# Threshold attention and a SoLU feed-forward on one core: three transfers for the weights' blocks, k and v loaded into all 128 rows

## The chip, the core and the metric

The kernel runs on one core of a Trainium2 chip. The metric is the device time of one execution in microseconds (us). Three executions of the kernel before gave 881.29, 881.4 and 883.73 us; the median, 881.4 us, is what the changed kernel is compared with.

The engines have short names here, as in the profile: PE is TensorE's matmul, PEld its load of the stationary operand, DVE is VectorE, ACT is ScalarE, POOL is GpSimd, SP is SyncE, which issues nearly all DMAs. A queue's name ends in q (SPq).

## The reference, cut to what matters

```python
# q, k, v: (8, 8, 576, 64) float32; tau = 0.02
scores = 0.125 * np.matmul(q, k.transpose(0, 1, 3, 2))
thresh = np.max(scores, axis=-1, keepdims=True) - tau
scores = np.where(scores >= thresh, scores, -1e9)
attn = np.exp(scores - np.max(scores, axis=-1, keepdims=True))
attn = attn / (np.sum(attn, axis=-1, keepdims=True) + 1e-09)
attn_out = np.matmul(attn, v)
x = attn_out.transpose(0, 2, 1, 3).reshape(4608, 512)
h = x @ w_in                         # (4608, 1024)
e = np.exp(h - np.max(h, axis=-1, keepdims=True))
solu = h * (e / (np.sum(e, axis=-1, keepdims=True) + 1e-9))
mu = np.mean(solu, axis=-1, keepdims=True)
var = np.mean((solu - mu) ** 2, axis=-1, keepdims=True)
out = (((solu - mu) / np.sqrt(var + 1e-6)) * g_ln) @ w_out   # (4608, 512)
```

## The kernel before

**Slots and rounds.** There are 8 batches (`b`) of 8 heads. Two heads make a pair; `NP` = 4 pairs per batch, numbered `hp`, and pair `i` is `b * NP + hp`. The 576 queries of a head are cut into two kinds of 256 (`kind` 0 and 1) and a rest of 64 (`kind` 2). A slot is one 128-row block of scores for both heads of a pair, and a batch has `PER` = 18 of them: 8 of kind 0, 8 of kind 1 and 2 of kind 2. One loop runs over rounds; a round issues, for all engines, the scores of one slot and whatever else is due. The order on each engine is the order in which this loop writes the instructions (the manual schedule), and each engine runs its queue strictly in order. Dates are in rounds: "round `PER * b - 9`" is nine rounds before the first slot of batch b.

**Attention of a slot.** PE makes the scores in PSUM (L451, tiles `s_ps`, one buffer for each head). DVE finds the row limit (L473), ACT makes the threshold ramp and the exponential (L488, L497), POOL normalises the rows (L504 to L507), and DVE transposes 32x32 blocks of the weights into `T` (L519). When both slots of a unit are in `T`, four DMAs on SP move the blocks from `T` to `wT` (L527 to L530), each from 32 partitions to 64 rows. Three rounds after the unit's second slot PE multiplies `wT` with `v` (L555, "pv"), and ACT copies the result into the tokens `xh`.

**Feed-forward.** A tile of 128 tokens takes `ff_h` (L611) and `ff_o` (L715) on PE, and between them DVE, ACT and POOL work and four DMAs on SP from `u` to `V` (`ff_swap`, L693), after which DVE makes `uT` (L703). A tile is begun about every fourth round.

**Inputs.** `q` is loaded for four heads at a time (L130) and turned by PE: `turn` (L312) multiplies with the identity matrix `ident`; `q_item` (L340) asks for it. For batches 0 and 1, `k` is turned the same way. From batch 2 on `load_natural` (L179) brings the `k` of one pair by four DMAs of 32 rows each (L186), `turn_natural` (L188) has DVE transpose it into `flip` (L191), and two DMAs put it into `kT` (L194). `v` of batches from 2 on is loaded by four DMAs for each half of a batch (L158), each two heads into 64 rows; rows 0 to 63 and 64 to 127 of `v` hold the same data, because PE uses both halves (`ROWS`). The rounds of these loads are worked out in L791 to L807. In batch 0 the sixteen pieces of `w_in` and `w_out` are also loaded as 64-bit numbers (L248) and turned into float32 by DVE, ACT and POOL (L259 to L298).

**Queues.** SP issues a round's DMAs in this order: `ff_swap` of the round, `wT` blocks of the slot before, output stores, `kT` halves, weight pieces, then `k`, `q` and `v` loads. A DMA whose input isn't ready holds back all behind it on SP. PE's order in a round is: the turns that ride on this slot, the scores, a quarter of the feed-forward, then pv.

## Time and profile before

| | |
|---|---|
| median of three runs | 881.4 us |
| the profiled execution's own time | 883.54 us |
| its span, first to last instruction | 881.8 us |
| mean granted TensorE clock | 0.980 |
| DMAs that SP issues: `wT`, `V`, `k`, `kT`, `v` | 288, 144, 96, 48, 48 (and 12 older `v` loads) |

The page's own head gives for each engine the time in which it was busy, and then the span in 40 equal slices of 22 us, one digit (tenths) a slice. The groups of instructions say how often a form ran, its mean time, and what ended the idle time just before it. Three of the groups around the change:

```profile
L519 DVE STREAM_TRANSPOSE T<-w 128x576 f32<-128x576 f32 x288 | 206.3, 752 | 7.4 <-POOL w L507 6.0
L703 DVE STREAM_TRANSPOSE uT<-V 128x1024 f32<-128x1024 f32 x36 | 44.5, 1236 | 23.7 <-DMA V<-u 23.5
L488 ACT ACTIVATE w<-s_ps,nth 128x576 f32<-128x576 f32 x280 | 199.8, 743 | 97.0 <-DVE nth L473 93.1
```

The first row reads: 288 transposes of 0.752 us took 206.3 us of DVE's span, and DVE stood idle for 7.4 us just before them, most of it until POOL had written the weights.

DVE's transpose of `k` (L191) takes 0.732 us. On SP, issuing took a median of 0.62 us for one `wT` DMA (mean 0.91), 0.45 (0.73) for one of `k`, 0.64 (0.94) for one of `v`, 0.58 (0.63) for one of `kT`. [...]

### The profile page before, as it was taken

How to read it: one execution, taken by the hardware profiler on the slowest of the kernel's cores; microseconds unless marked ns; L12 is line 12 of the kernel's file. 1: busy time of each engine (PE TensorE's matmuls, PEld its weight loads, DVE VectorE, ACT ScalarE, POOL GpSimd, SP SyncE). 2: the span in 40 equal slices, each digit the busy share in tenths (PEclk: the TensorE clock that was granted, in tenths of full speed). 3: DMA queues.
4: the chain of work that ended last, by engine and by line, in shares of the span. 5: the costliest groups of instructions: out<-in, count | busy, mean ns of one | idle time of the engine just before them, and what ended most of it. 6: DMA issues, size and time to landing. Idle time of an engine off the chain costs nothing. (4 is left out here: it accounts for less than half of the span.)

```text
span 881.8 us, 38016 instructions
## 1 busy us (share of the span) xinstructions
PE 835.4 (95%) x16225; PEld 592.1 (67%) x16225; DVE 682.0 (77%) x1248; ACT 586.3 (66%) x1201; POOL 471.0 (53%) x888
## 2 busy tenths in 40 slices
PE   5667999989999999999999999999999999999997
PEld 3445666665676877677777777777677677777655
DVE  5989788878787888888778887888687888777451
ACT  5977777767666766767677677777676777775121
POOL 2878655545555555555554655555555555555120
PEclk9878899999999999999999999999999999999999
DMA  7999978887878796988789787888779777866222
GB/s 230 254 260 256 218 186 196 217 191 175 201 170 212 178 208 157 206 207 189 158 194 214 184 204 166 208 213 185 165 173 219 182 174 155 186 133 143 65 49 49
DMA packets 85033, 161.60 MB, mean 183 GB/s; under 512 B 19832, under 2 KB 49536, under 8 KB 84864
## 3 DMA queue, kind: packets, MB, share of 16 engines
q1 hardware_dynamic: 83728, 157.18, 76.6%
q8 instruction: 127, 2.08, 1.1%
q10 hardware_dynamic: 1136, 2.00, 0.7%
q14 instruction: 42, 0.34, 0.1%
HBM read 46.14 MB, written 9.44 MB: 63 GB/s over the span
## 5 line engine op out<-in xcount | busy, mean ns | idle before, releaser
L473 DVE CUSTOM_DVE_ANT_0 w<-s_ps,tau_t 128x576 f32<-128x576 f32 x280 | 200.7, 754 | 108.0 <-PE s_ps L451 90.7
L715 PE MATMUL o_ps<-w,uT 64*64 64x256 f32 x4608 | 265.2, 376 | 1.1 <-DVE uT L703 1.1
L488 ACT ACTIVATE w<-s_ps,nth 128x576 f32<-128x576 f32 x280 | 199.8, 743 | 97.0 <-DVE nth L473 93.1
L715 PEld LDWEIGHTS o_ps<-w,uT 64*64 64x64 f32 x4608 | 218.9, 133 | 58.3 <-issue 13.8
L507 POOL TENSOR_SCALAR w<-w,sm 128x576 f32<-128x576 f32 x288 | 218.8, 772 | 14.3
L497 ACT ACTIVATE w<-w,ntau 128x576 f32<-128x576 f32 x288 | 220.3, 772 | 0.0
L611 PE MATMUL h_ps<-w,xh 64*64 64x512 f32 x1856 | 220.0, 596 | 0.0
L519 DVE STREAM_TRANSPOSE T<-w 128x576 f32<-128x576 f32 x288 | 206.3, 752 | 7.4 <-POOL w L507 6.0
L555 PEld LDWEIGHTS pv<-wT,v 64*64 64x64 f32 x5760 | 166.5, 136 | 51.1 <-issue 36.3
L451 PE MATMUL s_ps<-kT,qT 64*64 64x64 f32 (+1 forms) x2048 | 168.1, 422 | 16.4 <-ACT w L488 12.5
L555 PE MATMUL pv<-wT,v 64*64 64x128 f32 (+1 forms) x5760 | 170.9, 263 | 7.9 <-DMA wT<-T 3.7
L611 PEld LDWEIGHTS h_ps<-w,xh 64*64 64x64 f32 x1856 | 98.3, 135 | 96.6 <-issue 88.6
L504 POOL TENSOR_SCALAR sm<-sm 128x2 f32<-128x2 f32 x144 | 36.0, 250 | 229.5 <-ACT w L497 226.4
L505 POOL TENSOR_TENSOR sm<-sm,mone 128x2 f32<-128x2 f32 x144 | 104.6, 726 | 12.0
L677 ACT ACTIVATE V<-u,nb,rs 128x1024 f32<-128x1024 f32 x36 | 44.7, 1241 | 52.2 <-POOL nb L667 52.2
L451 PEld LDWEIGHTS s_ps<-kT,qT 64*64 64x64 f32 x2048 | 61.8, 139 | 25.1 <-ACT w L488 17.7
L578 ACT COPY xh<-pv 128x256 f32<-128x256 f32 x64 | 23.7, 370 | 67.3 <-PE pv L555 67.3
L703 DVE STREAM_TRANSPOSE uT<-V 128x1024 f32<-128x1024 f32 x36 | 44.5, 1236 | 23.7 <-DMA V<-u 23.5
L497 ACT ACTIVATION_READ_ACCUMULATOR w<-w,ntau 128x1 f32 x288 | 56.9, 198 | 0.0
L635 ACT ACTIVATE u<-h_ps,hm 128x1024 f32<-128x1024 f32 x36 | 40.2, 1118 | 21.2 <-DVE hm L626 15.3
L626 DVE TENSOR_REDUCE hm<-h_ps 128x1 f32<-128x1024 f32 x36 | 43.1, 1197 | 12.2 <-PE h_ps L611 6.2
L682 DVE TENSOR_SCALAR u<-u,rs,nb 128x1024 f32<-128x1024 f32 x36 | 42.4, 1178 | 12.7 <-ACT V L677 12.4
(82 smaller groups left out, 590.4 us busy)
## 6 DMA issues: line engine op xcount, KB each, us to landing
wT<-T SPq DMA_DIRECT2D x288, 288.0 KB, 5.9
v<-in_v_dram SPq DMA_DIRECT2D x48, 288.0 KB, 4.8
V<-u SPq DMA_DIRECT2D x144, 64.0 KB, 4.1
out_dram<-ob SPq DMA_DIRECT2D x71, 128.0 KB, 3.1
q<-in_q_dram SPq DMA_DIRECT2D x15, 512.0 KB, 5.9
k<-in_k_dram SPq DMA_DIRECT2D x96, 72.0 KB, 4.6
kT<-flip SPq DMA_DIRECT2D x48, 144.0 KB, 2.7
raw<-in_moe_w_out_dram SPq DMA_DIRECT2D x8, 512.0 KB, 8.2
```

Of the source, the lines that this page charges most:

```text
L451: nc.tensor.matmul(out=ps[h][ROWS[y], ks], lhsT=lhsT, rhs=d["kT"][ROWS[h], ks], start=True, stop=True,)
L473: nc.vector.tensor_tensor_reduce(out=w, in0=ps[:, 0:S], in1=(zero if loose else tau_t).to_broadcast([P, S]), scale=1.0, scalar=BIG, op0=AL ...
L488: nc.scalar.activation(out=d["w"][x], in_=d["w"][x] if d["loose"] else d["ps"][x][:, 0:S], func=AF.Prelu, bias=d["nth"][x], scale=-1.0, al ...
L497: nc.scalar.activation(out=w, in_=w, func=AF.Exp, bias=ntau, scale=1.0, accum_out=sm[:, x : x + 1])
L505: nc.gpsimd.tensor_tensor(out=sm, in0=sm, in1=mone, op=ALU.pow)
L507: nc.gpsimd.tensor_scalar(out=w, in0=w, scalar1=sm[:, x : x + 1], scalar2=1.0, op0=ALU.mult, op1=ALU.mult)
L519: nc.vector.transpose(out=T[:, :, r, h, :], in_=w)
L555: nc.tensor.matmul(out=to, lhsT=d["v"][ROWS[u], h0 + h, m ^ 4 * u if m < 8 and b < 2 else m], rhs=rhs, start=m == 0, stop=m == NK - 1,)
L611: mm = nc.tensor.matmul(out=h[ROWS[y], f], lhsT=x[ROWS[r], c, ROWS[y]], rhs=w1_parts[ROWS[r], c, part ^ r], start=part == 0 and c == 0, st ...
L677: nc.scalar.activation(out=V, in_=u, func=AF.Identity, bias=nb, scale=rs)
L703: nc.vector.transpose(out=uT, in_=d["V"].rearrange("p y (m x) -> p m y x", x=32))
L715: nc.tensor.matmul(out=d["o"][ROWS[z], 512 * r : 512 * r + 256], lhsT=d["uT"][ROWS[r], m].rearrange("p y x -> p (y x)"), rhs=w2[ROWS[r], m ...
```

## The change

Three things are changed.

1. **Blocks of weights.** For kinds 0 and 1 the four DMAs from `T` to `wT` become three: one takes partitions 32 to 95 and fills all 128 rows of `wT[:, 1]`, and two of 32 partitions fill the halves of `wT[:, 0]`. For this the 32-column halves of the queries of the second row half are exchanged: `turn` multiplies them with a new matrix `swapped` (two copies of `ident`'s blocks by POOL at the start) in place of `ident`. Kind 2 keeps its four DMAs.
2. **k from batch 2 on.** One DMA loads half the tokens (`a`) of two pairs into all 128 rows, 24 DMAs in place of 96. DVE's transposes stay 24, and the DMAs into `kT` 48; each transpose now serves half of two pairs. The rounds become `PER * b` - 9, - 7 (first two pairs) and - 1, + 1 (last two), with the loads three rounds before. Before they were - 13, - 9, - 5, - 1 for even batches from 4 on, - 11, - 7, - 3, + 1 for odd ones, and rounds 24, 30, 34, 39 for batch 2.
3. **v from batch 2 on.** Still four DMAs for a half batch, but of 576, 288, 144 and 144 KB in place of four of 288 KB: the first fills all rows for heads 0 and 2 (rows 64 to 127 get heads 1 and 3), the second one head slot with heads 1 and 2, the last two the rest. The matmul pv picks the head slot `(h0 + h - u) % 4`. The rounds are as before, but for one of the second half that moves from +6 to +5.

```diff
+    swapped = const.tile([P, 64], F32, name="swapped")
...
         if b > 1:
             if 0 in parts:
                 d["v"] = loads.tile([P, 4, NK, D], F32, tag="v", bufs=3, name="v")
+            to = d["v"].rearrange("p h m d -> p h (m d)")
+            rows = v_rows[64 * (H * b + 4 * hf) :][0:256]
             for part in parts:
-                two, u = divmod(part, 2)
-                nc.sync.dma_start(
-                    out=d["v"][ROWS[u], 2 * two : 2 * two + 2].rearrange("p h m d -> p h (m d)"),
-                    in_=v[b, hs][2 * two : 2 * two + 2].rearrange("h (p m) d -> p h (m d)", m=NK),
-                )
+                nc.sync.dma_start(**(
+                    dict(
+                        out=to.rearrange("p (e o) n -> p o e n", o=2)[:, 0],
+                        in_=rows.rearrange("(e r) n -> r e n", e=2),
+                    ),
+                    dict(out=to[:, 1], in_=rows[64:192]),
+                    dict(out=to[ROWS[1], 3], in_=rows[0:64]),
+                    dict(out=to[ROWS[0], 3], in_=rows[192:256]),
+                )[part])
             return
...
-    def load_natural(i):
-        b, hp = divmod(i, NP)
-        src = k[b, 2 * hp : 2 * hp + 2].rearrange("h (i a t) d -> a h i (t d)", a=2, t=NK)
+    k_rows = k.rearrange("b h (i a t) d -> a (b h i) (t d)", a=2, t=NK)
+    v_rows = v.rearrange("b h (p m) d -> (b h p) (m d)", m=NK)
+
+    def load_natural(i, a):
         raw = loads.tile([P, 4, 4, D], F32, tag="k", name="k")
-        natural[i] = raw = raw.rearrange("p h t d -> p (h t d)")[:, 0 : NK * D]
-        for g in range(4):
-            a, h = divmod(g, 2)
-            nc.sync.dma_start(out=raw[32 * g : 32 * g + 32], in_=src[a, h])
-
-    def turn_natural(i):
-        raw = natural.pop(i)
+        natural[i, a] = raw = raw.rearrange("p h t d -> p (h t d)")[:, 0 : NK * D]
+        nc.sync.dma_start(out=raw, in_=k_rows[a, 64 * i : 64 * i + P])
+
+    def turn_natural(i, a):
+        raw = natural.pop((i, a))
...
-        for a in range(2):
+        for j in range(2):
             nc.sync.dma_start(
-                out=to[:, 32 * NK * a : 32 * NK * (a + 1)],
-                in_=flip[ROWS[a]].rearrange("p g t x -> p g (t x)"),
+                out=pair(i + j)["kT"][:, 32 * NK * a : 32 * NK * (a + 1)],
+                in_=flip[ROWS[j]].rearrange("p g t x -> p g (t x)"),
             )
...
         make_identity(nc, ident)
+        for g in range(2):
+            of = 64 + 32 * (1 - g)
+            nc.gpsimd.tensor_copy(
+                out=swapped[ROWS[1], 32 * g : 32 * g + 32], in_=ident[ROWS[1], of : of + 32]
+            )
...
-                    out=spare[r][ROWS[y], to], lhsT=lhsT_of(r, y), rhs=ident[ROWS[r], ROWS[r]],
+                    out=spare[r][ROWS[y], to], lhsT=lhsT_of(r, y),
+                    rhs=swapped[ROWS[1]] if swap and r else ident[ROWS[r], ROWS[r]],
...
         to = wT.rearrange("p g m r h x -> p g (m r h x)")
+        if kind < 2:
+            nc.sync.dma_start(out=to[:, 1], in_=T[32:96])
+            for half in range(2):
+                nc.sync.dma_start(out=to[ROWS[half], 0], in_=T[96 * half : 96 * half + 32])
+            return
         for g in range(2):
...
-                            out=to, lhsT=d["v"][ROWS[u], h0 + h, m ^ 4 * u if m < 8 and b < 2 else m],
+                            out=to,
+                            lhsT=d["v"][
+                                ROWS[u], (h0 + h - u) % 4 if b > 1 else h0 + h,
+                                m ^ 4 * u if m < 8 and b < 2 else m,
+                            ],
...
-    for i in range(2 * NP, NPAIR):
-        b, hp = divmod(i, NP)
-        if b == 2:
-            at = (24, 30, 34, 39)[hp]
-        else:
-            at = PER * b + 4 * hp - (11 if b % 2 else 13)
-        turn_at[at] = i
-        load_at.setdefault(at - 3, []).append(lambda i=i: load_natural(i))
...
+    for i in range(2 * NP, NPAIR, 2):
+        b, hf = divmod(i // 2, 2)
+        for a in range(2):
+            at = PER * b + (-1 if hf else -9) + 2 * a
+            turn_at[at] = i, a
+            load_at.setdefault(at - 3, []).append(lambda i=i, a=a: load_natural(i, a))
...
+        for part, at in enumerate((4, 5, 5, 7) if hf else (-9, -7, -5, -3)):
+            load_at.setdefault(PER * b + at, []).append(
+                lambda b=b, hf=hf, part=part: load_v(b, hf, (part,))
+            )
```

## The prediction

> **What bounds the kernel now.** I read the page's head and slices first, then the time by stage, then who waited for whom on PE and DVE, and last the timeline of the one place where PE stands still in the steady part.

> ```profile
> span 881.8 us, 38016 instructions
> ...
> PE 835.4 (95%) x16225; PEld 592.1 (67%) x16225; DVE 682.0 (77%) x1248; ACT 586.3 (66%) x1201; POOL 471.0 (53%) x888
> ...
> PE   5667999989999999999999999999999999999997
> ...
> DMA  7999978887878796988789787888779777866222
> ...
> q1 hardware_dynamic: 83728, 157.18, 76.6%
> ...
> wT<-T SPq DMA_DIRECT2D x288, 288.0 KB, 5.9
> v<-in_v_dram SPq DMA_DIRECT2D x48, 288.0 KB, 4.8
> ```

> PE is full from the fifth slice on; before that, in the first 88 us, it is half to three quarters busy. The DMA engines are full in just that stage. The busy time by stage, in windows of 22 us, puts numbers to it (PE, PEld, DVE, ACT, POOL, then PE's granted clock, DMA share and GB/s):

> ```profile
> 22.00:44.00 22.00, 13.92 (x263) 8.87 (x261) 21.44 (x45) 19.81 (x44) 18.99 (x24) 0.84 1.02 253
> 44.00:66.00 22.00, 14.90 (x228) 10.04 (x224) 19.43 (x41) 15.68 (x33) 16.08 (x21) 0.75 1.04 260
> 66.00:88.00 22.00, 17.53 (x292) 12.25 (x284) 20.79 (x41) 16.74 (x35) 17.60 (x23) 0.89 1.06 258
> ...
> 176.00:198.00 22.00, 19.19 (x334) 14.34 (x330) 16.88 (x32) 13.73 (x29) 10.86 (x21) 0.92 0.86 192
> ...
> 484.00:506.00 22.00, 22.00 (x424) 15.56 (x420) 17.60 (x33) 15.41 (x32) 12.99 (x26) 1.00 0.76 185
> ```

> So there are two regimes. Until about 90 us DVE, which also converts the weights, is the bound, with the DMA engines saturated beside it. After that PE is: the last window stands for most of those that follow, with no idle time at all. PE's instructions are the same in number and shape after the change, so its busy time is a floor that DMAs can't move. Of PE's idle 881.8 - 835.4 = 46.4 us, the first 88 us hold 88 - (12.22 + 13.92 + 14.90 + 17.53) = 29.4 us (the first summand is the window from 0 to 22), and the end, from 858 us, holds about 6 us. Some 11 us lie between. What DMAs cost in waits:

> ```profile
> PE pv L555 <- DMA wT<-T: 3.7, 6, 1.3
> ...
> DVE em L259 <- DMA raw<-in_moe_w_out_dram: 1.6, 1, 1.6
> ...
> DVE em L259 <- DMA raw<-in_moe_w_in_dram: 0.5, 1, 0.5
> ...
> DVE uT L703 <- DMA V<-u: 23.5, 21, 4.1
> ...
> 179.87 0.33 PE L451 MATMUL s_ps<-kT,qT 64*64 64x64 f32 x4 [2.51 <-ACT qT L351]
> ...
> 181.44 5.38 PE L611 MATMUL h_ps<-w,xh 64*64 64x512 f32 x32
> ```

> The columns of a wait are us in total, times, longest. PE waited for blocks of weights only 3.7 us in all, 2.3 us of it between 44 and 88 us, where DVE is the bound anyway. DVE waited far more for `V` (23.5 us), but nearly always PE had work meanwhile. The last two lines are the exception: DVE was held up at 176.5 us by `V<-u`, which had come onto SP behind four k DMAs, one of v and one of q; so the limit, the ramp and the turned q came late, PE idled 2.51 us, and the 32 feed-forward matmuls after it took 5.38 us where the same form took 3.70 us at 173.66 us, at a clock that had dropped.

> [...]157.18 MB in 76.6% of 16 engines' 881.8 us is 157.18e6 / (0.766 x 16 x 881.8e-6) = 14.5 GB/s an engine[...].

> **The change part by part.**

> *Issues on SP.* `wT`: 64 units of kinds 0 and 1 lose one DMA each, k falls from 96 to 24, v stays at 48: 136 fewer. At the measured mean of 0.91 us (wT) and 0.73 us (k) that is 64 x 0.91 + 72 x 0.73 = 111 us of SP's queue. SP is not on the path, so this counts only where something urgent stands behind it.

> *Blocks of weights.* The bytes stay (1152 KB a unit); [...] I take 0.8 us. On the path this buys:
> - the two DVE waits for weight pieces, 2.1 us, in the saturated stage: pieces queue right behind the blocks. I take 1.5 us gained, bounds 0 and 2.1.
> - PE's waits for `wT` after 88 us, 3.7 - 2.3 = 1.4 us: I take 0.7, bounds 0 and 1.4. The other 2.3 us I count as nothing, since DVE covers them.

> *k and v.* The four k DMAs ahead of `V<-u` at 164 us were 3.3 us of SP's time; now k is loaded in rounds 24 and 26, away from that place (round 27). But v's first transfer there grows from 288 to 576 KB, and two `kT` halves (288 KB) join the round. At PE the stall was 2.5 us plus 5.38 - 3.70 = 1.7 us of slow clock, 4.2 us. Ahead of `V<-u` stood k, v and q, 288 + 288 + 512 KB; it will be kT, v and q, 288 + 576 + 512 KB[...]. I take 1.8 us gained; bounds: 4.2 gained, 1.5 lost.

> In later batches the round PER * b - 9 also has 288 KB more of v ahead of what follows: 288 KB / (16 x 14.5 GB/s) = 1.3 us later for it at the old rate[...]. I count 0, since PE idled at such places hardly at all and DVE has 22 - 17.6 = 4.4 us of slack in 22; without that cover it is up to 6 x 1.3 = 7.8 us.

> *Moved transposes.* 24 of 0.73 us on DVE before and after. They move to rounds - 9, - 7, - 1, + 1; the last half of `kT` is needed in round + 4, two whole rounds (about 11 us) after its transpose, against 2.7 us for the `kT` DMA to land. DVE has the slack just named. Cost 0, bounds - 1 and + 1.

> *Swapped matrix and new indices.* Two POOL copies of 64x32, estimated at 0.3 us each from the 0.29 us of the 128x128 select in the same place, end before 2.2 us; PE's first turn waits for k until 6.02 us. Same matmuls otherwise. Cost 0; uncovered, 0.6 us.

> *The end.* The last 70 us load no k and no v, and the closing chain runs through `V<-u`, which is untouched. Nothing.

> Sum: - 1.5 - 0.7 - 1.8 = - 4.0 us. Against the profiled execution's own 883.54 us (span 881.8 and 1.7 around it) that is 879.5 us. The median of the three runs lies 2.1 us lower, and the same difference from 881.4 us gives **877.4 us**. A difference under 0.3%, 2.6 us, can't be told from none here.

> **The rivals.**

> *Nothing shows.* The DMAs get faster, but PE is the bound and DVE the bound before it, so only a microsecond comes through: 880.4 us. For it: PE at 22.00 of 22 in window after window, and waits for `wT` of only 3.7 us. Against: the 4.2 us at 180 us, a DMA wait that did reach PE.

> *Slower by the crowded round.* In round PER * b - 9 two `kT` halves, v's 576 KB and q's 512 KB now stand together before the next `V<-u` or blocks. `uT` on DVE waits longer, all of DVE's later work with it, the ramp comes late and PE idles; once it idles for more than about 2.5 us, as at 180 us, the half clock adds 1.7. It decides from the point where `V<-u` is later than DVE's slack in a round, some 4.4 x 5.5 / 22 = 1.1 us. Price: 1.3 us for most of 6 batches, less what is covered, say 3.5, and one clock loss of 1.7: 886.6 us. For it: `uT` waited 21 times already, up to 4.1 us. Against: every wait of the steady part but one stayed off PE[...].

> *All of it.* [...]the stall at 180 us goes (4.2), the weight pieces' and blocks' waits go (3.5), and DVE starts the steady part sooner: 881.4 - 7.7 = 873.7 us.

> **How the numbers follow.** The forecast around 877.4 us has a chance of 0.42, all of it 0.06, nothing shows 0.28, the crowded round 0.24. Faster by over 0.3% is 0.42 + 0.06 = 0.48, within 0.3% 0.28, slower 0.24. The likeliest case alone spans 874.5 to 878.7 us. To hold 8 in 10 the range goes from 873 us, just under the full gain, to 885.5 us, which takes in the milder part of the crowded round.

> **What would show it.** Right: the DMA share of q1 falls by 5 points or more with the bytes unchanged; `wT` lands under 5.9 us; DVE's waits for weight pieces between 44 and 88 us and PE's wait near 180 us shrink, and the clock stays at 1.00 from 176 to 198 us. Wrong: the share stays at 76%[...]; DVE's wait for `V<-u` grows above 23.5 us and PE shows new waits for ACT after 200 us (the crowded round); or the clock drops in other places before 110 us, which moves the time without any of these steps.

## The result, and the profile after

The changed kernel took 889.0 us (median of 19 runs, 883.73 to 893.84) against 883.59 us of the kernel before (19 runs, 878.83 to 886.68) on the same chip: **1.0042 times the time before, 95% interval [1.0021, 1.0062]**. Two repetitions of the same kernel gave 1.0014 [0.9995, 1.0033] and 1.0035 [1.0013, 1.0057]. It is slower by 0.1 to 0.4% (one of the three intervals holds 1), where 877.4 us and a gain were forecast. The quotient of the two medians is 1.0061, at the upper end of the interval. Single executions of the kernel before ranged over 8 us beside these and over 12 us (876.94 to 888.92, without five slower ones of up to 891.87) beside the next; the three that were known beforehand ranged over 2.

The head of the page after the change, from a profiled execution of 893.84 us, the longest of the 19:

```profile
span 892.0 us, 37795 instructions
...
PE 836.6 (94%) x16225; PEld 589.5 (66%) x16225; DVE 676.8 (76%) x1248; ACT 587.3 (66%) x1201; POOL 474.8 (53%) x890
...
PE   5666899989999999999999999999899999999997
...
DMA  7999977777878786797778777796868776755322
...
q1 hardware_dynamic: 81552, 157.17, 71.6%
q8 instruction: 127, 2.08, 1.0%
...
wT<-T SPq DMA_DIRECT2D x160, 288.0 KB, 6.6
wT<-T SPq DMA_DIRECT2D x64, 576.0 KB, 5.4
```

The transfers did about what the prediction said of them. The same 157 MB fill 71.6% of the DMA engines' time in place of 76.6%, and a block transfer of 576 KB lands in 5.4 us where one of 288 KB took 5.9. The 288 KB transfers that are left take longer, 6.6 us, so the whole unit is what counts: from its first issue to its last landing, after 90 us, the median is 8.9 us in both traces of the kernel before and 8.1 to 8.5 us in the thirteen with the new blocks. PE's busy time is nearly unchanged: 836.6 us for 835.4. So 9 of the 10 us of this trace are idle time of PE. The time by stage (columns as before: PE, PEld, DVE, ACT, POOL, PE's clock, DMA share, GB/s) shows where it isn't:

```profile
176.00:198.00 22.00, 18.41 (x320) 12.21 (x316) 14.91 (x29) 14.12 (x32) 10.83 (x20) 0.92 0.82 222
...
484.00:506.00 22.00, 22.00 (x438) 15.60 (x434) 17.66 (x33) 15.61 (x33) 12.01 (x25) 1.00 0.68 161
```

The steady part is as full as it was. The stage from 176 to 198 us, whose stall was to vanish, is no better than before: PE busy 18.41 us for 19.19, at the same clock of 0.92 (the changed kernel is 7 us further behind in its work there). Who waited for whom, after the change (us in total, times, longest):

```profile
PE pv L574 <- DMA wT<-T: 6.3, 7, 1.8
...
DVE uT L726 <- DMA V<-u: 20.8, 17, 4.1
...
DVE em L270 <- DMA raw<-in_moe_w_out_dram: 3.2, 2, 2.1
```

In this trace the waits for blocks and weight pieces, which were to shrink, are 6.3 and 3.2 us, where they were 3.7 and 2.1; DVE's wait for `V`, which was to betray the crowded round, fell from 23.5 to 20.8. None of these sums tells the story. The same place in every trace does. So times are given from slot to slot here: "slot n" below is the time at which PE starts the scores of slot n, and the stretches between such times can be compared between kernels.

The place itself, on PE's timeline of the changed kernel:

```profile
187.14 0.33 PE L465 MATMUL s_ps<-kT,qT 64*64 64x64 f32 x4 [2.88 <-ACT qT L365]
187.77 2.03 PE L465 MATMUL s_ps<-kT,qT 64*64 64x64 f32 x12 [0.30 <-ACT w L502]
189.38 4.72 PE L634 MATMUL h_ps<-w,xh 64*64 64x512 f32 x32
```

PE stands 2.88 us before slot 31, and the 32 feed-forward matmuls that followed took 4.72 us (3.70 at full clock; 5.38 in the trace before), with a recorded clock of 0.50 from 188.0 to 191.4 us. DVE's timeline says why:

```profile
183.12 1.25 DVE L726 STREAM_TRANSPOSE uT<-V 128x1024 f32<-128x1024 f32 x1 [0.92 <-DMA V<-u]
184.29 0.73 DVE L198 STREAM_TRANSPOSE flip<-k 128x576 f32<-128x576 f32 x1
184.95 0.72 DVE L487 CUSTOM_DVE_ANT_0 w<-s_ps,tau_t 128x576 f32<-128x576 f32 x1
...
186.28 0.48 DVE L369 TENSOR_SCALAR qT<-s_ps,scl 128x256 f32<-128x256 f32 x1
```

`uT` waits 0.92 us for `V`; then comes a turn of k (`flip`, round 29), and only then the row limit (L487) for which ACT's ramp waits. ACT makes its part of `qT` behind that ramp, and PE waits for it. In the kernel before, the turn of round 30 came behind `qT` on DVE:

```profile
179.01 0.48 DVE L355 TENSOR_SCALAR qT<-s_ps,scl 128x256 f32<-128x256 f32 x1
180.75 0.74 DVE L191 STREAM_TRANSPOSE flip<-k 128x576 f32<-128x576 f32 x1
```

### The profile page after: what moved, and what is told of

The parts are those of the page before. It is cut to its first block, busy times and chain, and to the rows that moved or that the text cites. A ratio compares the mean times of both kernels' runs of the same rounds, so it can differ in the third digit from the quotient of the medians.

```text
span 892.0 us, 37795 instructions
## 1 busy us (share of the span) xinstructions
PE 836.6 (94%) x16225; PEld 589.5 (66%) x16225; DVE 676.8 (76%) x1248; ACT 587.3 (66%) x1201; POOL 474.8 (53%) x890
## 3 DMA queue, kind: packets, MB, share of 16 engines
q1 hardware_dynamic: 81552, 157.17, 71.6%
q8 instruction: 127, 2.08, 1.0%
## 5 line engine op out<-in xcount | busy, mean ns | idle before, releaser
L487 DVE CUSTOM_DVE_ANT_0 w<-s_ps,tau_t 128x576 f32<-128x576 f32 x280 | 200.4, 752 | 121.8 <-PE s_ps L465 102.3
L521 POOL TENSOR_SCALAR w<-w,sm 128x576 f32<-128x576 f32 x288 | 222.5, 784 | 14.3
L574 PEld LDWEIGHTS pv<-wT,v 64*64 64x64 f32 x5760 | 164.4, 135 | 52.6 <-issue 37.7
L465 PE MATMUL s_ps<-kT,qT 64*64 64x64 f32 (+1 forms) x2048 | 169.9, 426 | 18.5 <-ACT w L502 12.9
L574 PE MATMUL pv<-wT,v 64*64 64x128 f32 (+1 forms) x5760 | 168.3, 261 | 9.1 <-DMA wT<-T 6.3
L601 ACT COPY xh<-pv 128x256 f32<-128x256 f32 x64 | 23.7, 370 | 66.7 <-PE pv L574 66.7
L726 DVE STREAM_TRANSPOSE uT<-V 128x1024 f32<-128x1024 f32 x36 | 44.3, 1230 | 20.8 <-DMA V<-u 20.8
L664 DVE TENSOR_TENSOR u<-h_ps,u 128x1024 f32<-128x1024 f32 x36 | 42.8, 1189 | 10.8 <-ACT u L658 10.8
## 6 DMA issues: line engine op xcount, KB each, us to landing
wT<-T SPq DMA_DIRECT2D x160, 288.0 KB, 6.6
k<-in_k_dram SPq DMA_DIRECT2D x24, 288.0 KB, 5.3
```

What stands on the lines that cost most here:

```text
L465: nc.tensor.matmul(out=ps[h][ROWS[y], ks], lhsT=lhsT, rhs=d["kT"][ROWS[h], ks], start=True, stop=True,)
L487: nc.vector.tensor_tensor_reduce(out=w, in0=ps[:, 0:S], in1=(zero if loose else tau_t).to_broadcast([P, S]), scale=1.0, scalar=BIG, op0=AL ...
L521: nc.gpsimd.tensor_scalar(out=w, in0=w, scalar1=sm[:, x : x + 1], scalar2=1.0, op0=ALU.mult, op1=ALU.mult)
L574: nc.tensor.matmul(out=to, lhsT=d["v"][ROWS[u], (h0 + h - u) % 4 if b > 1 else h0 + h, m ^ 4 * u if m < 8 and b < 2 else m,], rhs=rhs, sta ...
L726: nc.vector.transpose(out=uT, in_=d["V"].rearrange("p y (m x) -> p m y x", x=32))
```

## The experiments

Three theories came first. **A**: the new blocks hurt the start, where the DMA engines are full (a share of 1.03 from 44 to 66 us; PE's `wT` waits at 76 us). **B**: the new loads of k and v crowd the rounds around `PER * b - 9`. **C**: PE stops at scattered places with no releaser, and the parts of the change matter little.

**One half at a time.** First kernel: blocks in three transfers with `swapped`, k and v as before. Second: the reverse. Third: the changed kernel with batch 0's blocks as before. Fourth: the changed kernel again.

```diff
# first: load_v, load_natural, turn_natural and their rounds as before
# second: wT as before, and no swapped columns
...
-        if kind < 2:
+        if kind > 2:
# third
-                    spare, x + t, lambda r, y: src["q"][ROWS[r], h0 + y, ts.start + t], swap=True
+                    spare, x + t, lambda r, y: src["q"][ROWS[r], h0 + y, ts.start + t], swap=i >= NP
...
-        if kind < 2:
+        if kind < 2 and b > 0:
```

> Only the three transfers of the weights' blocks and the swapped matrix; k and v are loaded as before. Theory A (the loss comes from the new blocks in the first 112 us, where the DMA engines are full: in the two profiles the changed kernel is 7.3 us behind at round 31, before any k or v of batch 2 is used): ratio 1.004 or more, scores of round 17 later than 109 us. Theory B (my rival, the crowded round PER*b-9): ratio 0.995 to 1.000, for the blocks alone take DMA time away. Theory C[...]: ratio anywhere between 0.998 and 1.004, with single PE waits for issue of 1 to 2 us at scattered places.

> Only the new loads of k and v from batch 2 on; blocks by four transfers and no swapped columns. Theory A: ratio 0.999 to 1.001, and everything before round 24 at the times of the kernel before, within 0.5 us. Theory B: ratio 1.004 or more, lost from round 27 on in steps of about 1 us a batch. Theory C: 0.998 to 1.004.

> The changed kernel, but batch 0 keeps four transfers for its blocks and unswapped columns. Theory A: the loss of the first 112 us is gone, ratio 0.998 to 1.001. Theory B: still 1.004. Theory C: between.

> The changed kernel once more, for a second profile of it. If the loss between rounds 12 and 17 (8 us in the first profile) and the waits for issue (6.9 us on PE against 2.3 us before) belong to the kernel, both are there again to within 1 us each; if they are chance of one execution, they differ by several us while the ratio stays near 1.004.

Measured: blocks alone **0.9946 [0.9925, 0.9967]**, k and v alone **1.0129 [1.0101, 1.0158]** (5 runs), batch 0 as before 1.0051 [1.0031, 1.0072], the changed kernel 1.0014. So the change is a gain and a loss, and A falls: the blocks are the gain. The changed kernel without them in batch 0 is 0.4% slower than with them (1.0051 against 1.0014), and still 0.8% faster than without any (1.0129). B, the crowded rounds, had the two signs right; where its loss lies is the next question. C is right in that PE stops at scattered places with no releaser (3.6 us in all in the second trace of the changed kernel, 6.8 in the first), but the parts of the change do matter. A part of the gain shows at the start. Slot 16 starts at 100.93, 104.44, 105.21 and 104.28 us in the four traces with old blocks in batch 0, and between 98.19 and 104.14 us, on average 100.55, in the twelve with new ones: some 3.2 us against the mean of 103.72, though the two groups overlap. PE's `wT` waits are there in these too (5.1 us with the blocks alone, nearly all between 61 and 77 us, where this trace was ahead of both traces of the kernel before).

Another part is at slot 31. The blocks alone, PE's timeline:

```profile
177.88 0.33 PE L458 MATMUL s_ps<-kT,qT 64*64 64x64 f32 x4 [0.92 <-ACT qT L358]
...
179.44 3.70 PE L623 MATMUL h_ps<-w,xh 64*64 64x512 f32 x32
```

A wait of 0.92 us, and full clock. The traces with the new k and v show 2.88 to 4.21 us instead (k and v alone 3.44), and slots 29 to 33 take 25.2 to 26.7 us in all four of them, against 21.50 with the blocks alone.

**What in k and v.** Four kernels, all with the new blocks: q of batch 2's second half one round later; the first two turns of batch 2, with the k loads and `kT` transfers that go with them, three rounds earlier; v as before; and q one round later with the old k and v.

```diff
# q later
-        load_at.setdefault(PER * (b - 1) + (9 if hf else -1), []).append(
+        load_at.setdefault(PER * (b - 1) + ((9 + (b == 2)) if hf else -1), []).append(
# turns earlier
-            at = PER * b + (-1 if hf else -9) + 2 * a
+            at = PER * b + (-1 if hf else -12 if b == 2 else -9) + 2 * a
```

> The changed kernel, with q of batch 2's second half (512 KB) asked for in round 28 in place of 27; nothing else differs. Theory D (one place: in round 27 SP holds kT until DVE has turned k, and v 576 KB and q 512 KB then stand right ahead of V<-u, so uT, the limit and the ramp come late): without q ahead of it V<-u lands about 2 us sooner (1088 KB less 512), PE's wait for ACT at the scores of slots 30 to 32 falls from 2.9-4.2 us to 1 us or less, no half clock follows, and the ratio to before is 0.994 to 0.998. Theory E (the new loads cost a little everywhere, [...]not there): the wait at 183 to 187 us may shrink, but the ratio stays at 1.000 to 1.004.

> The changed kernel, with the two k loads and turns of batch 2's first half three rounds earlier (turns in 24 and 26 in place of 27 and 29), so that no kT transfer that waits for DVE, and no turn of 0.7 us, stands in round 27; v and q stay there. Theory D, where kT's wait for DVE is what holds v and q back: PE's wait at slots 30 to 32 falls to about before's 2.5 us or under and the ratio is 0.995 to 0.999. If the bytes of v and q alone do it, the wait stays at 2.5 us or more with half clock after it, and the ratio stays at 0.999 to 1.003. Theory E: ratio 1.000 to 1.004, whatever the wait does; the turn could also meet a busier DVE in round 24 and cost 1 us there.

> The changed kernel with v as before (288 KB for each two heads' half, four transfers of 64 rows); blocks in three transfers and k for two pairs stay. It parts v's share from k's. Theory D: in round 27 v is 288 KB and not 576, so V<-u lands up to 1.2 us sooner than in the changed kernel (at 14.5 GB/s an engine), the wait at slots 30 to 32 is 1.5 to 2.5 us, and the ratio is 0.995 to 0.999. If k's new place in round 27 is the whole cost, the ratio stays at 1.001 to 1.004; if v's 576 KB is, it falls to 0.994 to 0.996, as with the blocks alone.

> Blocks in three transfers with k and v as before, and q of batch 2's second half asked for in round 28 in place of 27: the candidate that should beat both. Theory D: the last 0.9 us of PE's wait at slots 30 to 32 goes too, and the ratio is 0.992 to 0.995, at or just under that of the blocks alone (0.9946). Theory E says nothing of it: 0.994 to 0.996; if q then collides with the blocks of round 28, 0.996 to 0.998.

| kernel | ratio | PE's wait at slot 31 | slots 29 to 33 |
|---|---|---|---|
| q later | 0.9994 [0.9976, 1.0012] | 2.35 us | 25.90 us |
| turns earlier | 0.9981 [0.9958, 1.0005] | 0.93 us | 21.65 us |
| v as before | 1.0009 [0.9987, 1.0031] | 2.74 us | 25.09 us |
| blocks alone, q later | 0.9943 [0.9911, 0.9974] | 0.92 us | 23.94 us (2.3 of them a stop with no releaser, below) |

The early turns decide. Theory D, that the transfers crowd ahead of `V<-u`, had forecast 1 us or less for q later, and missed; it also missed with v as before. For the earlier turns its forecast held. With these three rounds earlier the whole loss at this place is gone, though v's 576 KB and q's 512 KB still stand where they did. (The edit moves `kT`'s transfers too, so how much is the turns on DVE and how much `kT` on SP it doesn't say.) DVE's timeline of that kernel:

```profile
174.14 1.20 DVE L726 STREAM_TRANSPOSE uT<-V 128x1024 f32<-128x1024 f32 x1
175.27 0.72 DVE L487 CUSTOM_DVE_ANT_0 w<-s_ps,tau_t 128x576 f32<-128x576 f32 x1
...
176.60 0.48 DVE L369 TENSOR_SCALAR qT<-s_ps,scl 128x256 f32<-128x256 f32 x1
```

`uT` no longer waits, and from its start to that of `qT` are 2.46 us, where the changed kernel has 3.16: the turn's share. Giving v back its old shape does nothing (2.74 us): the bytes of v, at which the prediction had looked, are not it. Taking q away shortens `uT`'s wait to 0.39 us but leaves both turns on DVE, and half clock still follows the wait of 2.35 us (25.90 us for slots 29 to 33). Blocks with q later is no better than the blocks alone: its ratio fell into D's range, but the wait of 0.92 us, which D said would go, stayed. These two beat the kernel before by 0.5%. The kernel with earlier turns, at 0.9981, lies 0.35% above them; the intervals overlap, so whether it pays for something else too isn't shown.

**Order on SP, and which batches.** In the changed kernel SP issues in round 27:

```profile
173.79 1.20 SPq L200 DMA_DIRECT2D kT<-flip  x2
175.04 1.20 SPq L160 DMA_DIRECT2D v<-in_v_dram  x1
176.28 0.47 SPq L131 DMA_DIRECT2D q<-in_q_dram  x1
176.85 2.51 SPq L716 DMA_DIRECT2D V<-u  x4
```

`kT` goes out when DVE's turn has ended (it starts at 173.03 us and takes 0.74); v and q come behind `kT`, and `V<-u`, at 176.85 us, right behind them. Of four more kernels the first puts v and q ahead of `kT`; the second and third load k and v the new way only from batch 3 on, or only in batch 2; the fourth is the kernel before, for a second trace.

```diff
# loads first
-            if rnd in turn_at:
+            if rnd in turn_at and rnd != 27:
                 turn_natural(*turn_at[rnd])
...
             for job in load_at.pop(rnd, []):
                 job()
+            if rnd == 27:
+                turn_natural(*turn_at[rnd])
```

> The changed kernel, with only the order of issue in round 27 altered: v and q are put on SP ahead of the two kT transfers that wait for DVE's turn; the turn keeps its place on DVE and every byte its round. Theory D1 (SP's in-order wait holds v and q back until V<-u is due): uT's wait for V<-u falls from 2.24 us to under 1 us and PE's wait at slots 30 to 32 from 4.21 us to 2.2 to 2.6 us (0.92 as with the blocks alone, and 0.65 us for each of the two turns that now stand ahead of qT on DVE), probably still with half clock; ratio 0.998 to 1.001. Theory D2 (bytes, not their order): uT's wait stays at about 2 us, the gap at 3.5 us or more, ratio 1.001 to 1.004.

> Blocks in three transfers; batch 2 loads k and v as before, in its old rounds, and only batches 3 to 7 load them the new way. Theory D (the whole loss lies in batch 2, at slots 30 to 32): the wait there is 0.9 us with full clock after it and the ratio is that of the blocks alone, 0.993 to 0.996. Theory F (the 0.35% by which the kernel with the earlier turns, 0.9981, stands above the blocks alone, 0.9946, lies in the later batches): 0.997 to 0.999.

> The complement: blocks in three transfers, batch 2 loads k and v the new way in the new rounds, batches 3 to 7 as before. Theory D: the wait of 2.7 to 4.2 us at slots 30 to 32 with half clock after it is back, and the ratio is that of the changed kernel, 1.000 to 1.004. Theory F: part of the loss stays behind, 0.997 to 1.000.

> The kernel before itself, as a second trace and as a measure of what two equal programs differ by here. Ratio 1.000, between 0.998 and 1.002. If PE's wait of 2.51 us near 180 us and the half clock after it belong to the program, the second trace shows a wait of 2.3 to 2.7 us there; if they were chance, about 1 us, and then what the blocks gained there was chance too.

Loads first: 1.0003 [0.9977, 1.003], and `uT` still waits 1.24 us (PE's own wait, 0.70 us, can't be read: a stop of 2.28 us with no releaser had held PE up in slot 29). D1 expected under 1, D2 about 2; since the changed kernel itself shows 0.92 to 2.24, this decides nothing: whether SP's order matters stays open. The batches: from batch 3 on **0.9950 [0.9930, 0.9969]**, with slots 29 to 33 at 21.48 us; batch 2 only 0.9979 [0.9961, 0.9997], with 24.78 us: the loss is in its place, but the ratio lies below D's range and in that of its rival F. So beside the new blocks the later batches' new loads cost nothing that shows, although there too v's 576 KB and the `kT` halves share a round: the loss that these kernels show is in batch 2.

Beside the old blocks it is not. Of the 1.3% (11 us) that k and v alone cost, slots 29 to 33 hold some 2 us in its trace, and slots 54 to 143 some 7 us: 501.0 us, against 493.7 and 494.5 in the two traces of the kernel before. In that stretch PE waits for `uT` in slots 61, 97 and 133, 0.7 to 1.4 us each, and over the whole trace DVE's wait for `V` has grown from 23.5 to 37.0 us:

```profile
DVE uT L726 <- DMA V<-u: 37.0, 24, 4.1
561.97 3.68 PE L738 MATMUL o_ps<-w,uT 64*64 64x256 f32 x64 [1.40 <-DVE uT L726]
```

This is what the rival of the crowded round had foreseen, in one trace, and no run takes it apart. In the three traces of the changed kernel, which has the new blocks too, the wait for `V` is 20.8, 20.5 and 23.7 us.

The kernel before against itself gave 1.0000 [0.9980, 1.0021], and corrected a reading of mine. Its second trace:

```profile
182.16 0.33 PE L451 MATMUL s_ps<-kT,qT 64*64 64x64 f32 x4 [1.30 <-ACT qT L351]
...
183.71 3.70 PE L611 MATMUL h_ps<-w,xh 64*64 64x512 f32 x32
```

The wait is 1.30 us, not 2.51, and the clock holds (3.70 us for the 32 matmuls, not 5.38). Of the 4.2 us that I had put down to the stall before, a good part was one execution's bad luck.

**Is it all of batch 2's cost, and do the parts add up?**

> As the kernel in which only batch 2 loads k and v the new way, with batch 2's first two turns three rounds earlier (24 and 26). Theory D (the two turns and the kT transfers in rounds 27 to 29 are the whole cost of the new loads): slots 29 to 33 take 21.5 to 21.7 us, as with the blocks alone, in place of 24.78, and the ratio is 0.993 to 0.996. If something else in batch 2's new loads costs too, 0.996 to 0.998.

> The changed kernel once more, beside the kernel with the new loads in batch 2 alone. If the parts add up (0.9950 for batches 3 to 7 alone, 0.9979 for batch 2 alone, 0.9946 for neither), the ratio is 0.998 to 1.000. If the two together cost more than their sum, it is again 1.001 to 1.004. In the trace slots 29 to 33 take 24.8 us or more either way; if the ratio is above 1.001, the stretch that holds the rest is looked for between slots 16 and 29 and after slot 40.

Batch 2 alone with its turns earlier: **0.9952 [0.9934, 0.9971]**, slots 29 to 33 at 21.63 us. The early turns, with their `kT` transfers, are all that batch 2's loads cost. The changed kernel: 1.0035, so the parts don't add up to it (0.9950 and 0.9979 with 0.9946 for neither make 0.998). One place where all three traces of the changed kernel are longer than those before lies between slots 16 and 29: 73.67, 69.35 and 69.90 us, against 67.24 to 67.25 for both traces before. In each of them PE stops in slot 22 for 1.3 to 1.9 us, with nothing to wait for that the profile shows; the first and the third:

```profile
105.07 4.92 PE L634 MATMUL h_ps<-w,xh 64*64 64x512 f32 x26 [1.75 <-issue]
...
142.79 3.02 PE L738 MATMUL o_ps<-w,uT 64*64 64x256 f32 x49 [1.84 <-issue]
```

```profile
141.84 3.02 PE L738 MATMUL o_ps<-w,uT 64*64 64x256 f32 x49 [1.86 <-issue]
```

The first trace has one more such stop, at 105 us, with half clock after it (26 matmuls in 4.92 us). In the records of the DMA queues a 16 KB packet of `q8`, the queue that the page calls `instruction`, ends 1.4 to 1.6 us before PE goes on in slot 22 (in the two shown it started at 139.6 and 139.3 us and was 1.61 and 1.03 us long). The kernels with q later and with loads first are the same as the changed kernel, instruction by instruction, up to round 27, and took 67.63 and 67.27 us there without that stop. So the change's transfers up to there don't suffice to bring it. Two of the ten other kernels with new blocks show it as well (0.74 us from batch 3 on, 1.86 us in batch 2 with earlier turns). The second of these has the same 69.90 us between slots 16 and 29 and is at 0.9952 all the same, so the stop doesn't tell the slow kernel from the quick ones. Why the changed kernel showed it three times in three, and what makes the 0.3 to 0.6% between 0.998 and what was measured, stays open.

## Why the prediction was wrong

- **k and v: "I take 1.8 us gained; bounds: 4.2 gained, 1.5 lost".** This is the step that failed, and with the next one it makes the sign wrong. The new loads cost 1.3% beside the old blocks (1.0129) and 0.7 to 1.0% beside the new (1.0014 to 1.0042 over 0.9946). Slots 29 to 33 of the changed kernel take 25.23, 26.56 and 25.94 us in three traces, on average 25.9, against 24.76 and 21.85 before, 23.3: 2.6 us lost in place of 1.8 gained, and 4.4 us lost against the blocks alone. I had counted the bytes ahead of `V<-u`. About as much again of the loss (0.3 to 0.6%) has no place yet.
- **"Moved transposes ... Cost 0, bounds - 1 and + 1".** The other half of the same error. Turns moved to rounds 27 and 29 fall ahead of the normalised `u` and of the limit that `qT` waits behind, 0.66 us each; I covered them by DVE's slack of 4.4 us in a window at 484 us. In the round in question PE waits for what DVE makes, and that slack doesn't exist. With the later `V` the wait grows, and the clock falls after it: all nine traces with 2.35 us or more at slot 31 lost a further 1.3 to 2.9 us to the half clock there, and none with 1.30 us or less had it there. It lasted 3.4 us there (3.41 in the first trace of each kernel; twice 6.8). At other places it followed shorter stops (figures in the last section).
- **Crowded round in later batches, "I count 0".** Right beside the new blocks: 0.9950 from batch 3 on. Beside the old ones it would have been wrong (7 us in slots 54 to 143 of k and v alone). The rival of the crowded round had the sign and the 1.7 us of clock right, but for the changed kernel it spread the price over six batches, where the loss that was found is at one place. Its 5.2 us lie near the 5.4 us between the measured medians; with the blocks' gain left out of it, that is luck.
- **Blocks: - 1.5 and - 0.7 us.** Right in kind, too small: the whole is 0.54%, or 4.8 us of 885. By the traces about 3.2 us of it come before slot 16 (upper bound given: 2.1) and 0.4 to 3.3 us at slots 29 to 33, by which of the two traces before one compares. My estimate that a unit lands 0.8 us sooner, which rested on no measurement, was good (0.4 to 0.9). The named carriers were wrong: neither the waits for weight pieces nor PE's for `wT` shrank reliably. Nor did SP gain time by it: a unit's three issues took 3.5 to 3.6 us in all, as its four had (3.6).
- **DMA share down by 5 points, bytes unchanged.** Right: 76.6 to 71.6%; the blocks alone account for most (72.4%). That is 15.4 GB/s an engine (157.17 MB in 71.6% of 16 engines' 892.0 us) in place of 14.5; why the new shapes move their bytes in less of the engines' time was not shown, and a smaller share is no gain by itself.
- **The base.** The two numbers that a profile gives of a stall, 2.51 and 1.7 us, came from one execution; the other one has 1.30 and none.

## What to carry to other kernels

A moved instruction of 0.7 us is not free because its engine has slack on average: look at what stands behind it in its queue at its new place, and whether PE waits for that. A transfer that is quicker by itself can be worth its 0.5% (the blocks) while the rescheduling that comes with it loses it again; put the two in separate kernels, and the two together, before judging either: here the loads cost 1.3% beside the old blocks and 0.7 to 1.0% beside the new. A stall seen in one trace should be seen in a second before its removal is priced.

## What the runs showed of the hardware

**Stops of PE with no releaser.** The `q8` row, of the kind `instruction`, holds 127 packets of 16 KB, 2.08 MB, one about every 7 us, 1.17 us long on average; whose instructions they carry it doesn't say. In sixteen traces PE's waits with no releaser sum to between 0.9 us (batch 0's blocks as before) and 8.2 us (loads first), in single stops of up to 2.3 us, and they recur at a few places of the stream (slots 19, 22, 75 and 111 to 112 among them), though not in each execution. Of the 39 stops of over 0.7 us, 32 ended 1.2 to 1.8 us after a packet of `q8` had (in the first trace of each kernel all five, by 1.3 to 1.6 us); the other seven, all in slot 19 and of 1.1 us, ended 2.8 to 3.5 us after one, and may have another cause. That PE waits for these packets is not shown. The sums are as large as the effects of this whole change.
